# Loads of a tile's upper partitions issued by ACT, and a later start for the loads of weights

## The chip, the cores and the metric

The kernel runs on one core of a Trainium2 chip. The metric is the device time of one execution in microseconds (us); the time of a kernel is the median over several runs.

## The reference, cut to what matters

Three layers follow one another: attention in chunks with a few memory keys, a mixture of experts in which each token goes to two of eight, and a second one in which each token goes to one of eight.

```python
# attention: batch 4, heads 8, 768 positions, head size 64, chunks of 32
for c in range(nc):
    q_c = q[:, :, c_start:c_end]
    k_full = np.concatenate([mem_k, k[:, :, l_start:r_end]], axis=2)   # 16 left, 8 right, 8 memory keys
    v_full = np.concatenate([mem_v, v[:, :, l_start:r_end]], axis=2)
    scores = scale * np.matmul(q_c, k_full.transpose(0, 1, 3, 2))
    a = np.exp(scores - np.max(scores, axis=-1, keepdims=True))
    out[:, :, c_start:c_end] = np.matmul(a / (a.sum(-1, keepdims=True) + 1e-09), v_full)
x = out.transpose(0, 2, 1, 3).reshape(3072, 512)
# experts 1: noisy top 2 of 8;   h = max(x[mask] @ w1[e], 0);  out[mask] += weight * (h @ w2[e])
# experts 2: the largest of 8;   h = max(x[mask] @ w1[e], 0);  out[mask] = gate * (h @ w2[e])
```

## The kernel before

**Attention.** The 3072 tokens are 24 tiles of 128 tokens (NT = 24). The host lays out, for each tile, everything that attention needs of q, k and v in five arrays, `xa` to `xe`, and `load(t)` brings them into one of five buffers `X[t % LK]` (LK = 5) with five DMAs, all issued by SyncE: `xa` to partitions 0 to 31, `xb` to 32 to 63, `xc` to 64 to 127, `xd` to 64 to 95 and `xe` to 96 to 127. In a row they fill 2288, 1508, 736, 1552 and 772 floats. Two heads share the 128 partitions, and the columns hold the values (VN = 1040 for either half), the keys and the queries; what a half does not use is cleared once for each buffer by `clear` (VectorE and GpSimd), and `spread(t)` copies parts of the values along partitions on GpSimd.

**The order of the loop.** The loop over `t` is written out by hand and runs from 0 to 25; each engine executes its own instructions in this order. In iteration `t` stand: `clear(t + 1)` for the first buffers; `scores(t)`, 32 matmuls and on VectorE the maximum and the subtraction; `flip(t - 1)`, the transposes of the exponentials and their copy `et` on ACT; `exp(t)` on ACT; a step of the router `route` (VectorE above all) for a batch of six tiles; `values(t - 2)`, 32 matmuls, then `load(t + 3)` into the buffer that these matmuls were the last to read, then the division on VectorE, the split into a high and a low float16 part (VectorE, then GpSimd's subtraction), and the store of the tile to `X16` by SyncE; `spread(t)`; `turn(t - 3)`, the transposes of the tile and the copy `xt` on ACT; `logits(t - 4)`. So a load waits on its queue for the matmuls of `values`, and a store for GpSimd's subtraction. The loads of tiles 0 to 4 are issued ahead of the loop, and ACT then issues two small loads (noise and the router's weights).

**Zeroes and `wide`.** At `t == 2` VectorE writes a table `wide` for the router and a tile of zeroes, and SyncE stores the zeroes to the scratch tensors `L` (two stores) and `G`.

**Weights.** `Weights` brings the experts' weights in pieces of 128 partitions by 1024 floats (512 KB) into four staging buffers. `fill` issues loads, by SyncE, while fewer than `depth` pieces are staged; `high` converts a piece on ACT (L127) and `low` on VectorE (L128), and frees the buffer. In attention `depth` begins to grow at `t == 14`, by one in each iteration up to 4. The first conversion stands at `t == 24`.

**After attention** come the two mixtures of experts, matmuls of tokens gathered by GpSimd's DMAs; the change leaves their code alone.

Of the kernel before, what the change touches and what calls it, by code (L numbers as in the profile page):

```python
# [23 lines left out]
QN, KN, VN = 512, 736, 1040  # L24
QK = QN + KN
VC = VN // 4
XK, XQ, XU, XV = VN, VN + KN, VN + QK, VN + QK + QN
# [227 lines left out]
class Attention:  # L255
# [30 lines left out]
    def load(self, t):  # L286

        x = self.X[t % LK]  # L290
        for i, (p, n, o, e) in enumerate(((0, 32, 0, XU), (32, 32, 3 * VC, XU), (64, 64, XK, XQ),
                                          (64, 32, XU, XV + VN), (96, 32, XU, XV + VC))):
            self.nc.sync.dma_start(x[p:p + n, o:e], self.qkv[i][t])

    def spread(self, t):

# [925 lines left out]
def build(tc, xa, xb, xc, xd, xe, noise, wr, wg2, w1, w2, v1, v2, out):  # L1222
    nc = tc.nc
    with ExitStack() as top:
# [18 lines left out]
        def src(e):  # L1243
            v = (w1[e].rearrange("(p k) f -> p (k f)", k=4), w2[e].rearrange("(p k) d -> p (k d)", k=8))
            return lambda i, c: v[i][:, c * 1024:c * 1024 + 1024]

        with ExitStack() as ctx:
            wk = ctx.enter_context(tc.tile_pool(name="wk", bufs=2))
            ld = ctx.enter_context(tc.tile_pool(name="ld", bufs=1))
            at = Attention(tc, g, (xa, xb, xc, xd, xe), ld, wk)  # L1250
            at.ps = ctx.enter_context(tc.tile_pool(name="psa", bufs=1, space=PSUM))
            at.load(0)
            nc.scalar.preload_act_table_set("natural_log_exp_and_others")
            gates = at.gates(noise, wr)
            at.clear(0)
            constants(tc, g, ld)
            for t in range(1, LK):
                at.load(t)
            route = None
            for t in range(NT + 2):  # L1260
                if t + 1 < LK:
                    at.clear(t + 1)
                if t == 0:
                    next(gates)
                if t == 3:
                    at.wrh = next(gates)
                if t == 2:
                    g.wide = g.c.tile([128, 128, M], F16, name="wide")
                    nc.vector.tensor_copy(g.wide, g.iota[:, 0:128, None].to_broadcast([128, 128, M]))
                    z = ld.tile([128, NT * E], F32, name="zero")  # L1270
                    nc.vector.memset(z, 0.0)
                    for u in range(2):
                        nc.sync.dma_start(g.L.rearrange("(u p t) x -> u p (t x)", u=2, p=128)[u], z)
                    nc.sync.dma_start(g.G.rearrange("(p t) x -> p (t x)", p=128), z[:, 0:2 * NT])
                if t >= 14:
                    W.depth = min(W.depth + 1, 4)
                    if t == 14:
                        for e in range(E):
                            W.add((1, e), src(e))
                    W.fill()  # L1280
                if t < NT:
                    at.scores(t)
                if 0 < t <= NT:
                    at.flip(t - 1)
                if t < NT:
                    at.exp(t)
                if route and t < 25:
                    for _ in range(2 if t in (17,22) else 1):
                        next(route, None)
                if t >= 2:  # L1290
                    at.values(t - 2)
                if t < NT:
                    at.spread(t)
                if 0 <= t - 3 < NT - 2:
                    at.turn(t - 3)
                if t >= 4:
                    at.logits(t - 4)
                if t >= 4 and (t - 4) % TB == TB - 1:
                    route = at.route((t - 4) // TB)
                    next(route)  # L1300
                if t == 20:
                    m1 = Moe1(tc, g, dr)
                    m1.gather(0)
                if t == 22:
                    for b in range(m1.preps(0)):
                        m1.prep(0, b)
                if t >= 24 and W.may():
                    W.high()
                    W.low(nc.vector)
            m1.gates(0)  # L1310
# [143 lines left out]
def layouts(inp):  # L1454
    import numpy as np
    f = np.float32


    def split(x, y):

        return x.reshape(B, 2, 2, 2, *y)

    def pad(a):
        p = np.zeros((B, H, S + 40, D), f)
        p[:, :, 16:16 + S] = a
        return p
    q = split(inp["q"], (TB, 4, 32, D)).transpose(0, 4, 2, 7, 6, 1, 3, 5).reshape(NT, 128, QN)
    p = pad(inp["k"])
    k = np.stack([np.concatenate([x for c in range(4) for x in (p[:, :, 128 * j + 32 * c:128 * j + 32 * c + 32],
                                                                 inp["mem_k"])]  # L1470
                                 + [p[:, :, 128 * j + 128:128 * j + 152]], axis=2) for j in range(TB)], axis=2)
    k = split(k, (TB, KN // 4, D)).transpose(0, 4, 2, 6, 1, 3, 5).reshape(NT, 128, KN)
    p = pad(inp["v"])

    def values(w, c):

        w = split(w, (TB, c, 32, D)).transpose(0, 4, 3, 6, 5, 1, 2, 7)
        v = np.ones(w.shape[:-1] + (D + 1,), f)
        v[..., :D] = w
        return v.reshape(NT, 64, c * VC)  # L1480
    va = values(p[:, :, :S], 4)
    vb = values(np.concatenate([x for j in range(TB) for x in (p[:, :, 128 * j + 128:128 * j + 152], inp["mem_v"])],
                               axis=2), 1)
    seq = [b * TB + j for b, j in SEQ]
    k, q, va, vb = k[seq], q[seq], va[seq], vb[seq]
    vu = va[:, 32:].reshape(NT, 32, 4, VC)[:, :, ::-1].reshape(NT, 32, VN)
    qkv = [np.concatenate(x, axis=2) for x in ((va[:, 0:32], k[:, 0:32], q[:, 0:32]),
                                               (vb[:, 0:32], k[:, 32:64], q[:, 32:64]), (k[:, 64:],),
                                               (q[:, 64:96], vu), (q[:, 96:], vb[:, 32:]))]

    def rows(w):

        w = w.reshape(E, 4, 128, 128, 8).transpose(0, 2, 1, 4, 3)
        return np.ascontiguousarray(w).reshape(E, DM, F)

    def gate(w):
        return w.reshape(4, 128, -1).transpose(1, 0, 2).reshape(128, -1)
    return {
        **{"x" + "abcde"[i]: x for i, x in enumerate(qkv)},
        "noise": inp["moe_noise"].reshape(NT, 128, E)[seq].transpose(1, 0, 2).reshape(128, NT * E),  # L1500
        "wr": gate(np.concatenate([inp["moe_w_gate"], inp["moe_w_noise"]], axis=1)),
        "wg2": gate(inp["moe2_w_gate"]),
        "w1": rows(inp["moe_w1"]), "w2": inp["moe_w2"], "v1": rows(inp["moe2_w1"]), "v2": inp["moe2_w2"],
    }
# [30 lines left out]
```

## Time and profile before

| | |
|---|---|
| time, median of 3 runs | 1029.54 us (1027.92 to 1031.64) |
| the profiled execution's own time | 1027.09 us |
| its span in the profile | 1025.3 us |
| attention in it, first to last scores | 8.5 to 132 us |
| TensorE busy over the span | 952.6 us (93%) |
| VectorE, ACT, GpSimd busy | 49%, 38%, 47% |

The span is the time from the first to the last profiled instruction of one execution; the execution's own time has what lies around it as well. PE is TensorE, DVE VectorE, ACT ScalarE, POOL GpSimd, SP SyncE. The busy share is an average over stages with different limits, and a busy TensorE is not one at its peak, so the stage has to be read by itself.

### The profile page before, as it was taken

The numbers are of one execution on the slowest core, as the hardware profiler recorded it, in microseconds if no ns is written. First come the engines' busy times: TensorE is split into PE (matmuls) and PEld (weight loads), VectorE is DVE, ScalarE is ACT, GpSimd is POOL, SyncE is SP. The second block draws the span as 40 slices with busy tenths as digits, with TensorE's granted clock in tenths as the row PEclk, the third lists the DMA queues.
The fourth block names the chain that finished last, engine by engine and source line by source line (L and its number), as shares of the span: only waits on it lengthen the run. The fifth ranks groups of instructions, "written<-read, shape, count | busy, mean of one in ns | idle before, by whom it ended". The sixth has DMA issues, their size and how long they took to land.

```text
span 1025.3 us, 18840 instructions
## 1 busy us (share of the span) xinstructions
PE 952.6 (93%) x7303; PEld 568.2 (55%) x7303; DVE 499.7 (49%) x1032; ACT 386.0 (38%) x653; POOL 478.1 (47%) x484
## 2 busy tenths in 40 slices
PE   5898958999989999989999999998888998999998
PEld 4777845656545555445555555553464564555665
DVE  7689886642423443234233433483574265455511
ACT  2444444322423343234333333254324254445421
POOL 6755562334545454636455455345217245434321
PEclk9998979999999999999999999999989999999999
DMA  9999959745747686668668766498246689988720
GB/s 205 259 260 241 249 132 283 186 88 125 183 111 171 164 183 162 149 157 190 158 156 180 159 158 140 100 321 220 54 162 191 163 211 254 272 161 267 148 58 19
DMA packets 189218, 180.75 MB, mean 176 GB/s; under 512 B 152148, under 2 KB 153044, under 8 KB 188352
## 3 DMA queue, kind: packets, MB, share of 16 engines
q1 hardware_dynamic: 166736, 131.24, 54.6%
q0 software_dynamic: 21952, 48.07, 16.0%
q8 instruction: 60, 0.98, 0.4%
q14 instruction: 38, 0.31, 0.1%
q10 hardware_dynamic: 432, 0.15, 0.1%
HBM read 118.27 MB, written 39.53 MB: 154 GB/s over the span
## 4 chain that ended last, share of the span: by engine, by line
PE 30%; issue 13%; POOL 6%; DMA 5%; DVE 4%; ACT 1%; POOLq 0%; SPq 0%; DVEq 0%; ACTq 0%
PE ph L543 14%; PE py L554 14%; POOL x L1042 2%; POOL out_dram L1061 1%; DMA stage<-in_v_dram 1%; DMA Y<-y,t3y 1%; POOL xp L1014 1%; POOL gs L1014 1%; DMA xt<-x 1%; DVE w L128 1%; ACT w L127 1%; DMA xp<-Y,ter 1%; DMA xp<-Y,tbr 1%; DVE hT L546 1%; DVE ol L507 0%
## 5 line engine op out<-in xcount | busy, mean ns | idle before, releaser
L543 PE MATMUL ph<-xT,w 128*128 128x384 f16 (+3 forms) x2688 | 426.8, 318 | 26.4 <-DVE hT L546 15.5
L554 PE MATMUL py<-w,hT 128*128 128x512 f16 x1800 | 394.4, 379 | 1.4 <-ACT hT L545 1.1
L543 PEld LDWEIGHTS <-w 128*128 128x128 f16 x2688 | 262.9, 99 | 172.1 <-issue 29.8
L554 PEld LDWEIGHTS <-hT 128*128 128x128 f16 x1800 | 175.4, 98 | 209.2 <-ACT hT L545 1.6
L546 DVE SCALAR_TENSOR_TENSOR hT<-ph,hT 128x384 f16<-128x384 f32 (+3 forms) x224 | 115.6, 520 | 218.0 <-ACT hT L545 216.7
L128 DVE SCALAR_TENSOR_TENSOR w<-stage,w 128x1024 f16<-128x1024 f32 x128 | 165.9, 1300 | 72.8 <-ACT w L127 72.4
L545 ACT ACTIVATE hT<-ph 128x384 f16<-128x384 f32 (+3 forms) x224 | 103.1, 462 | 206.1 <-PE ph L543 205.8
L127 ACT ACTIVATE w<-stage 128x1024 f16<-128x1024 f32 x128 | 133.5, 1049 | 24.0 <-DMA stage<-in_v_dram 20.6
L654 ACT ACTIVATE y<-py,gs 128x512 f32<-128x512 f32 x48 | 32.9, 686 | 177.2 <-PE py L554 166.7
L675 DVE SCALAR_TENSOR_TENSOR x<-y,x 128x512 f16<-128x512 f32 x50 | 34.4, 688 | 123.8 <-ACT x L671 123.8
L657 POOL DMA_INDIRECT L<-l,t3y x43 | 44.7, 1038 | 98.7 <-DVE l L686 95.3
L657 POOL DMA_INDIRECT Y<-y,t3y x43 | 44.1, 1027 | 98.7 <-ACT y L654 88.2
L1061 POOL DMA_INDIRECT out_dram<-y,tbo x22 | 23.0, 1048 | 126.4 <-ACT y L1060 108.3
L316 PE MATMUL s<-x 128*64 128x64 f32 x768 | 49.5, 289 | 17.5 <-DMA x<-in_xe_dram 11.5
L611 POOL DMA_INDIRECT Y<-ol,late x48 | 56.0, 1166 | 16.4 <-issue 16.4
L316 PEld LDWEIGHTS s<-x 128*64 128x64 f32 x768 | 46.1, 208 | 19.0 <-POOL x L303 8.5
L1060 ACT ACTIVATE y<-py,gs 128x512 f32<-128x512 f32 x27 | 18.5, 686 | 90.6 <-PE py L554 59.9
L370 POOL TENSOR_TENSOR x<-x,x 128x512 f16<-128x512 f32 x24 | 29.5, 1228 | 47.2 <-DVE x L369 25.0
L585 POOL DMA_INDIRECT xg<-X,t3x x43 | 42.0, 978 | 15.1 <-issue 14.6
L585 POOL DMA_INDIRECT gs<-G,t3g x41 | 38.7, 944 | 12.5 <-issue 12.5
L1042 POOL TENSOR_TENSOR x<-xp 128x512 f32<-128x512 f32 x27 | 36.9, 1389 | 13.5 <-DVE xg L1045 9.9
L303 POOL COPY x<-x 24x780 f32<-24x780 f32 x48 | 41.0, 854 | 3.9 <-issue 1.3
(276 smaller groups left out, 702.1 us busy)
## 6 DMA issues: line engine op xcount, KB each, us to landing
stage<-in_w_dram SPq DMA_DIRECT2D x64, 512.0 KB, 4.9
stage<-in_v_dram SPq DMA_DIRECT2D x64, 512.0 KB, 5.9
x<-in_xa_dram SPq DMA_DIRECT2D x24, 286.0 KB, 8.2
X<-x SPq DMA_DIRECT2D x24, 256.0 KB, 4.8
x<-in_xd_dram SPq DMA_DIRECT2D x24, 194.0 KB, 5.9
x<-in_xb_dram SPq DMA_DIRECT2D x24, 188.5 KB, 5.0
x<-in_xc_dram SPq DMA_DIRECT2D x24, 184.0 KB, 7.5
x<-in_xe_dram SPq DMA_DIRECT2D x24, 96.5 KB, 7.2
```

The source lines that it names most:

```text
L127: nc.scalar.activation(hi, src, AF.Copy, scale=SW)
L128: return lambda v=nc.vector: v.scalar_tensor_tensor(lo, src, SW, hi, op0=OP.mult, op1=OP.subtract)
L303: self.nc.gpsimd.tensor_copy(x[p + 32:p + 56, d:d + 3 * VC], x[p:p + 24, s:s + 3 * VC])
L316: nc.tensor.matmul(s[o:o + 64, ch // 2, b], q[:, b, ch], k[:, b, 40 * ch:40 * ch + 64], start=True, stop=True)
L543: nc.tensor.matmul(p[:, :n], w1[:, a, k, f, :], xT[:, b, k, :n], start=(i == 0), stop=(i == 11))
L545: nc.scalar.activation(hT[:, 0, f, :n], p[:, :n], AF.Relu)
L546: nc.vector.scalar_tensor_tensor(hT[:, 1, f, :n], p[:, :n], 0.0, hT[:, 0, f, :n], op0=OP.max, op1=OP.subtract)
L554: nc.tensor.matmul(p[:m], hT[:, a, f, o:o + m], w2[:, c, f, :], start=(i == 0), stop=(i == 23))
L585: self.nc.gpsimd.indirect_dma_start(out=out, out_offset=None, in_=src, in_offset=IO(ap=idx, axis=0))
L611: st = nc.gpsimd.indirect_dma_start(out=self.Y, out_offset=IO(ap=idx[:, i:i + 1], axis=0), in_=z, in_offset=None, bounds_check=2 * N - 1, ...
L657: st = nc.gpsimd.indirect_dma_start(out=dst, out_offset=IO(ap=idx, axis=0), in_=src, in_offset=None, bounds_check=2 * N - 1, oob_is_err=False)
L1042: nc.gpsimd.tensor_tensor(s, x[:, :DM], x[:, DM:], op=OP.add)
```

## The change

In `load`, the three DMAs to partitions 64 to 127 are issued by ACT (`nc.scalar`), the two to partitions 0 to 63 by SyncE as before. The five stand in another order, in which the halves alternate, and the host's arrays are renamed to fit: `xb` is now what goes to partitions 64 to 95, `xc` what goes to 32 to 63, `xd` what goes to 64 to 127. What is transferred is the same. `wide` and the zeroes move from the iteration `t == 2` to `t == 6`. The loads of weights begin at `t == 18` instead of `t == 14`.

```diff
-        for i, (p, n, o, e) in enumerate(((0, 32, 0, XU), (32, 32, 3 * VC, XU), (64, 64, XK, XQ),
-                                          (64, 32, XU, XV + VN), (96, 32, XU, XV + VC))):
-            self.nc.sync.dma_start(x[p:p + n, o:e], self.qkv[i][t])
+        for i, (p, n, o, e) in enumerate(((0, 32, 0, XU), (64, 32, XU, XV + VN), (32, 32, 3 * VC, XU),
+                                          (64, 64, XK, XQ), (96, 32, XU, XV + VC))):
+            (self.nc.scalar if p >= 64 else self.nc.sync).dma_start(x[p:p + n, o:e], self.qkv[i][t])
...
-                if t == 2:
+                if t == 6:
                     g.wide = g.c.tile([128, 128, M], F16, name="wide")
...
-                if t >= 14:
+                if t >= 18:
                     W.depth = min(W.depth + 1, 4)
-                    if t == 14:
+                    if t == 18:
                         for e in range(E):
                             W.add((1, e), src(e))
...
-                                               (vb[:, 0:32], k[:, 32:64], q[:, 32:64]), (k[:, 64:],),
-                                               (q[:, 64:96], vu), (q[:, 96:], vb[:, 32:]))]
+                                               (q[:, 64:96], vu),
+                                               (vb[:, 0:32], k[:, 32:64], q[:, 32:64]),
+                                               (k[:, 64:],), (q[:, 96:], vb[:, 32:]))]
```

## Rows read from the trace of the kernel before

**Rows 1.** The page: DMA share in 40 equal slices of the span, in tenths.

```profile
DMA  9999959745747686668668766498246689988720
```

**Rows 2.** Stretches: busy us (instructions) by engine; then granted clock, DMA share, GB/s.

```profile
core 0: us, PE busy (x) PEld busy (x) DVE busy (x) ACT busy (x) POOL busy (x), PEclk, DMA share, GB/s
10.00:15.00 5.00, 2.55 (x43) 2.33 (x40) 2.90 (x5) 0.81 (x3) 4.70 (x6) 1.00 1.04 221
15.00:20.00 5.00, 3.64 (x41) 3.09 (x39) 4.25 (x9) 1.41 (x4) 1.55 (x2) 1.00 1.03 219
...
40.00:60.00 20.00, 20.00 (x388) 17.92 (x390) 13.46 (x31) 10.74 (x24) 14.31 (x16) 1.00 1.03 279
...
125.00:147.00 22.00, 13.66 (x263) 11.31 (x259) 20.07 (x66) 11.28 (x21) 14.02 (x13) 0.92 0.42 112
...
158.00:160.00 2.00, 2.00 (x19) 1.95 (x18) 1.84 (x3) 1.61 (x4) 0.00 (x0) 1.00 0.96 391
```

**Rows 3.** DMA issues from 152 to 160 us: KB each, median us to landing.

```profile
stage<-in_w_dram SPq DMA_DIRECT2D x5, 512.0 KB, 6.8
```

**Rows 4.** Waits of TensorE, to 36 us and from 36 to 131: us, times, longest.

```profile
PE s L316 <- DMA x<-in_xe_dram: 11.0, 2, 8.5
PE s L316 <- DMA x<-in_xd_dram: 5.1, 2, 3.7
...
PE misc L227 <- DVE two L428: 3.4, 1, 3.4
...
PE s L316 <- DMA x<-in_xd_dram: 0.8, 1, 0.8
PE s L316 <- DMA x<-in_xe_dram: 0.5, 1, 0.5
```

**Rows 5.** Timeline of TensorE: start, us, scores of tiles 0, 1, 2, 4, 5, 11.

```profile
8.51 2.09 PE L316 MATMUL s<-x 128*64 128x64 f32 x32 [8.51 <-DMA x<-in_xe_dram]
13.05 2.08 PE L316 MATMUL s<-x 128*64 128x64 f32 x32 [2.45 <-DMA x<-in_xe_dram]
...
17.54 2.10 PE L316 MATMUL s<-x 128*64 128x64 f32 x32 [1.36 <-DMA x<-in_xd_dram]
...
29.71 2.07 PE L316 MATMUL s<-x 128*64 128x64 f32 x32 [3.70 <-DMA x<-in_xd_dram]
...
35.17 2.05 PE L316 MATMUL s<-x 128*64 128x64 f32 x32
...
61.20 2.08 PE L316 MATMUL s<-x 128*64 128x64 f32 x32
```

**Rows 6.** Timeline of the links between those scores.

```profile
12.28 0.81 ACT L333 ACTIVATE e<-d 128x256 f32<-128x256 f32 x3 [10.23 <-DVE d L325]
...
15.06 1.12 PE L340 MATMUL pt<-ident,e 128*128 128x128 f32 x4
...
20.59 1.09 PE L356 MATMUL o<-x,et 128*32 128x130 f32 x32
...
23.49 1.16 POOL L370 TENSOR_TENSOR x<-x,x 128x512 f16<-128x512 f32 x1 [6.89 <-DVE x L369]
...
28.27 1.38 POOL L277 MEMSET x<- 64x1552 f32 x1
```

**Rows 7.** SyncE's issues: loads 15 and 25; then all of a kind, ns min/median/max.

```profile
10.63 0.31 SPq L293 DMA_DIRECT2D x<-in_xe_dram  x1
...
19.49 0.31 SPq L293 DMA_DIRECT2D x<-in_xe_dram  x1
...
L293 SPq DMA_DIRECT2D x<-in_xc_dram x24: 471/471/567, 1.7 to 121.2; - x24
L293 SPq DMA_DIRECT2D x<-in_xd_dram x24: 310/576/1280, 2.3 to 121.9; - x24
L293 SPq DMA_DIRECT2D x<-in_xe_dram x24: 310/419/608, 2.9 to 123.0; - x24
```

**Rows 8.** Timeline: the fourth load of weights, and the first conversions on ACT.

```profile
101.94 0.42 SPq L74 DMA_DIRECT2D stage<-in_w_dram  x1
...
140.94 1.99 ACT L127 ACTIVATE w<-stage 128x1024 f16<-128x1024 f32 x2
```

## The prediction

> **What bounds the kernel now.** I read the page first, then tables by stretch of time, then the waits of TensorE, then the timeline of the first 40 us. The page's row of DMA shares stands at 9 in the first five slices of 25.6 us: attention is the stage in which the DMA engines are full, and nothing later in the span is so for long [rows 1]. The change touches only this stage, from 0 to about 147 us.
>
> The table by stretch splits the stage. From 10 to 20 us nothing but loads of tiles is under way: 221 and 219 GB/s at a DMA share of 1.04 and 1.03, while TensorE works 2.55 and 3.64 us of 5. From 40 to 60 us TensorE is busy for all 20.00 us and the DMA share is 1.03 as well, now at 279 GB/s with the stores among the loads. From 125 to 147 us VectorE is busy 20.07 of 22 us and the DMA share is 0.42 [rows 2]. The reader is to see three bounds in turn: loads, then TensorE with the DMA just keeping up, then VectorE.
>
> One row decides what a faster load could be. From 158 to 160 us the traffic is loads of weights over all 128 partitions [rows 3], and they move 391 GB/s at a share of 0.96 [rows 2]. The loads of tiles, each within partitions 0 to 63 or 64 to 127, keep the engines as busy and move 220: the same engine takes nearly twice as long over each byte. So the limit of the first 20 us is not the number of busy engines; it goes with the half that is written.
>
> The waits of TensorE agree. Up to 36 us it waited for loads alone, 11.0 and 5.1 us; from 36 to 131 us only 0.5 and 0.8 us, and longer for VectorE, 3.4 us once [rows 4]. The timeline places them: scores of tile 0 start at 8.51, tile 1 at 13.05, tile 2 at 17.54 us, each released by a load, then tile 4 only at 29.71 and tile 5 at 35.17. From there no gap until tile 11 at 61.20: six tiles, 26.03 us, 4.34 us each [rows 5].
>
> **The change, part by part.** *Issue.* A tile is (32·2288 + 32·1508 + 64·736 + 32·1552 + 32·772)·4 B = 0.972 MB, and the two halves have 0.486 MB each. Three of its five loads go to ACT's queue. No byte is added. SP is relieved of, and ACT charged with, the medians of those three issues: 0.471 + 0.576 + 0.419 = 1.47 us a tile [rows 7].
>
> What it gains is a rate that the trace does not show: two queues, each confined to its half. Lower bound 220 GB/s (the two queues together do what one did), upper bound 391 (each half runs as alone, up to what a load over all partitions reached) [rows 2]. The engine that waits on one half can find a packet for the other in the second queue, which speaks for the upper row; that the packets alternate evenly is not shown, which speaks against its full value. I take the middle, 305. A tile then takes 0.972/0.305 = 3.19 us instead of 0.972/0.220 = 4.42, so 1.23 us less.
>
> Scores of tile 2 need three tiles: 3·1.23 = 3.7 us earlier. From there to tile 4 the chain is engine work in a fixed order: transposes, values of tile 0 at 20.59, GpSimd's subtraction at 23.49, four spread copies, the clearing of buffer 4 at 28.27 for 1.38 us, scores at 29.71 [rows 5, 6]. GpSimd had idled 6.89 us before 23.49, so it can start earlier, and all links move together: 3.7 us. At 391 GB/s the loads would give 3·(4.42 − 2.49) = 5.8, but scores of tile 1, then at 13.05 − 3.9 = 9.2, and the 2.08 and 1.12 us behind them keep tile 2 from starting before 12.4, which leaves 5.1. Both ends: 0 and 5.1.
>
> *Does it last?* From tile 5 TensorE needs a tile every 4.34 us. A tile and its store of 0.262 MB at 391 GB/s (0.67 us) take 4.42 + 0.67 = 5.09 us now, which only the five tiles loaded ahead make good, and 3.19 + 0.67 = 3.86 at 305. It lasts if the rate is above 0.972/(4.34 − 0.67) = 265 GB/s. Past 61 us the stage is paced by VectorE; there only the waits of 0.5 and 0.8 us for loads go [rows 4]: 1.3 us.
>
> *ACT.* Its work is 10.74 us in 20 [rows 2], 2.33 a tile; (20/4.34 = 4.6 tiles); with 1.47 it is 3.80, under 4.34. Break-even is (4.34 − 2.33)/3 = 0.67 us an issue; the longest on SP took 1.28, behind a full queue [rows 7]. A load of tile t+3 waits on ACT for the matmuls of values of tile t−2, and behind it stand the copy of the transposed tile, the next copy of `et` and the next exp. Those matmuls start as soon as the transposes of the tile are done, before that tile's exp has its input, so I cost the wait at nothing; what hides it is VectorE's maximum and subtraction. Without that cover it is a part of the 1.09 us of those matmuls. SP keeps the stores behind the other two loads and loses only entries.
>
> *Zeroes and `wide`*, from the third to the seventh tile: one copy, one memset and three small stores move on VectorE and SP. VectorE is busy 4.25 us of 5 at the old place and 13.46 of 20 at the new [rows 2]. Nothing either way, bounds plus and minus 1 us.
>
> *Weights.* Four loads of 512 KB move by four tiles; the fourth now goes out at 101.94 us and ACT first touches one at 140.94 [rows 8]. Some 20 us later is still early enough, under the cover of the last tiles. They leave tiles 17 and 20, whose waits I have counted, and meet tiles 20 to 23: nothing at 305 GB/s, but at 220 they cost there what they save before.
>
> *Sum.* 3.7 + 1.3 = 5.0 us. The profiled execution took 1027.09 us around a span of 1025.3; 1027.09 − 5.0 = 1022.1. The median of the runs is 2.45 above that execution, so 1024.5. What follows attention starts earlier by as much, with its order unchanged.
>
> **Rivals.** *The two queues do as one.* The busy share is 1.03 already [rows 2]; if engines meet at the same half at the same time, as they must when loads of one half are all that one queue holds, a second queue only changes the order. Then nothing is gained: 1029.5. Against it: the engines are free to be out of step, and with stores among the loads the rate was 279. This is also what the Trainium skill says: SBUF — State Buffer, section "Can I just issue two DMAs to hit both halves?", has two concurrent loads at partitions 0 and 64 only 6% faster than one, and DMA: Bandwidth & Descriptors, section "Issuing engines are not separate DMA queues", has a second issuing engine save only issue time. By that the rate would be 233 GB/s, the three tiles 0.8 us earlier and the time 1028.8. No run here shows it yet; the port table that the Trainium skill has on the first of these pages, section "Door 1: The DMA port swizzle (why `[64,N]` ≈ `[32,N]`)", by which either half reaches half of the ports, agrees with 220 against 391 [rows 2].
>
> *ACT is held at the head of its stream*, the one that ends on the other side. All fifteen loads of tiles 0 to 4 on ACT stand ahead of its first exp, which started at 12.28 us. SP issued its fifteenth load at 10.63 but its last, of tile 4, at 19.49, held back by a full queue [rows 6, 7]. If ACT is held as long, exp ends at 20.6, the first transposes start there instead of at 15.06, and scores of tile 2 follow 1.1 later, at 21.8 instead of 17.54: 4.2 us late, down the same chain. Time 1033.7. It decides once exp starts after 15.6 us (17.54 − 1.12 for the transposes − 0.81 for itself). For it: the issues of a full queue. Against: ACT's queue holds 128 rows a tile, not 192, and drains faster if the rate rises.
>
> *ACT becomes the bound.* At 0.9 us an issue ACT has 2.33 + 2.7 = 5.03 us a tile, 0.7 over TensorE, on six tiles 4.1 us: it eats the 3.7, and the time is about 1028.6.
>
> **Numbers.** Forecast 0.55, queues as one 0.25, ACT held 0.13, ACT the bound 0.07. A difference under 0.3%, 3.1 us, can hardly be told from none in runs that lie 3.7 us apart (1027.92 to 1031.64). The forecast's own range goes from 1022.0 (5.1 + 1.3, and 1.1 because tile 4 need not take 35.17 − 29.71 = 5.46 us but 4.34) to 1026.0 (265 GB/s: 3·0.75 + 1.3). The whole range takes in two things more. If the chain between tiles 2 and 4 does not stay whole and TensorE alone paces it from 12.4 us on, tile 5 starts at 12.4 + 3·4.34 = 25.4 instead of 35.17; with the 1.3 that is 11.1 us, 1018.4, and less the 1.6 us by which the fastest run shown lies under the median, about 1017. Above, queues as one with the 2.1 us by which the slowest lies over it give 1032; most of the ACT-held case is left out. Faster 0.55; same 0.27 (queues as one, and a little of ACT as the bound); slower 0.18 (ACT held, the rest).
>
> **What would show it.** In the stretch from 5 to 15 us, over 265 GB/s at a share of about 1; scores of tile 2 before 15 us and of tile 5 near 31.5; tiles 5 to 11 still 4.34 us apart; exp of tile 0 before 12.3; no waits of TensorE for tiles 17 to 23. Wrong at the first step: 220 GB/s and tile 2 at 17.5. Wrong at ACT: exp of tile 0 after 15.6, issues of 0.7 us and more, or gaps of TensorE that `et` ends.

## Result, and the profile after

The change made the kernel slower by half a per cent: 1033.18 us against 1026.88 us (medians of 20 runs each), a ratio of 1.0057, 95% interval 1.0039 to 1.0076. One of the changed kernel's runs took 1932.45 us, where the other 19 lie between 1028.40 and 1041.41, and the ratio is without it (the median of the 19 is 1032.71). The forecast was 1024.5, its range ended at 1032. The profiled execution of the changed kernel took 1041.41 us and so lies 8 us over its own median; what it shows of the first 156 us is used here, what it loses after them is not put down to the change (from the first expert matmul to the last it took 877.7 us, before 872.8).

Stretches of the changed kernel, with the columns of [rows 2]:

```profile
10.00:15.00 5.00, 2.46 (x40) 2.12 (x36) 3.71 (x7) 0.00 (x0) 4.70 (x5) 1.00 1.02 222
15.00:20.00 5.00, 0.00 (x0) 0.00 (x0) 0.00 (x0) 0.37 (x2) 1.38 (x1) 1.00 1.03 229
...
40.00:60.00 20.00, 17.60 (x345) 15.76 (x342) 13.59 (x28) 9.19 (x20) 14.46 (x15) 1.00 0.96 257
125.00:147.00 22.00, 16.82 (x294) 14.26 (x287) 18.52 (x66) 10.82 (x25) 14.88 (x16) 0.84 0.81 212
```

Two things are to be seen. The loads hardly went faster: 222 and 229 GB/s at a share of 1.02 and 1.03, where [rows 2] have 221 and 219. And from 15 to 20 us TensorE and VectorE did nothing at all and ACT 0.37 us, while the loads went on. TensorE's waits to 36 us and from 36 to 131 us (as in [rows 4]):

```profile
PE s L316 <- DMA x<-in_xe_dram: 8.3, 1, 8.3
PE pt L340 <- ACT e L333: 6.9, 1, 6.9
PE s L316 <- POOL x L277: 5.0, 2, 3.9
...
PE misc L227 <- DVE two L428: 4.0, 1, 4.0
PE xp L383 <- ACT xt L384: 2.6, 3, 1.4
```

The loads are waited for once, for tile 0. The 6.9 us for ACT's exp and the 2.6 us for its copy `xt` are new. ACT's timeline (DMA issues and the first exp) shows why:

```profile
16.58 0.32 ACTq L293 DMA_DIRECT2D x<-in_xe_dram  x1
18.74 0.36 ACTq L283 DMA_DIRECT2D noi<-in_noise_dram  x1
19.14 0.45 ACTq L247 DMA_DIRECT2D wrf<-in_wr_dram  x1
19.63 0.81 ACT L333 ACTIVATE e<-d 128x256 f32<-128x256 f32 x3 [15.93 <-DMA x<-in_xb_dram]
```

The first exp starts at 19.63 us instead of 12.28 [rows 6], behind ACT's fifteenth load of a tile and two small loads. The scores follow (tiles 1, 2, 4, 5, 7, 8, 9; compare [rows 5]):

```profile
11.52 2.06 PE L316 MATMUL s<-x 128*64 128x64 f32 x32 [1.12 <-POOL x L277]
21.54 2.11 PE L316 MATMUL s<-x 128*64 128x64 f32 x32
...
34.00 2.12 PE L316 MATMUL s<-x 128*64 128x64 f32 x32 [3.89 <-POOL x L277]
39.67 2.04 PE L316 MATMUL s<-x 128*64 128x64 f32 x32
...
48.33 2.04 PE L316 MATMUL s<-x 128*64 128x64 f32 x32
53.68 2.04 PE L316 MATMUL s<-x 128*64 128x64 f32 x32
59.48 2.04 PE L316 MATMUL s<-x 128*64 128x64 f32 x32
```

Tile 1 is 1.5 us early, tile 2 is 4.0 us late, tile 5 4.5 us late. Then tiles 7 to 8 and 8 to 9 take 5.35 and 5.80 us instead of 4.34. That is where the zeroes now stand, in the changed kernel's timeline of SyncE and of ACT:

```profile
48.23 1.22 SPq L1273 DMA_DIRECT2D L<-zero  x2
49.50 1.69 SPq L1274 DMA_DIRECT2D G<-zero  x1
```

```profile
50.04 1.16 ACTq L293 DMA_DIRECT2D x<-in_xd_dram  x1
51.24 0.60 ACTq L293 DMA_DIRECT2D x<-in_xe_dram  x1
51.88 1.02 ACT L384 ACTIVATE xt<-xp 128x1024 f16<-128x1024 f16 x1 [2.73 <-POOL x L370]
...
56.53 0.47 ACTq L293 DMA_DIRECT2D x<-in_xd_dram  x1
...
57.68 1.02 ACT L384 ACTIVATE xt<-xp 128x1024 f16<-128x1024 f16 x1 [3.59 <-PE o L356]
```

Issues are stretched on both engines, and the copy `xt` stands behind ACT's. TensorE's transposes wait for that copy in both tiles, 2.4 of the 2.5 us that these two tiles lose:

```profile
52.96 0.61 PE L383 MATMUL xp<-ident,x 128*128 128x128 f16 x8 [0.97 <-ACT xt L384]
...
58.76 0.61 PE L383 MATMUL xp<-ident,x 128*128 128x128 f16 x8 [1.43 <-ACT xt L384]
```

At tile 23 the kernel is 8.8 us late (scores at 139.0 against 130.2), at the first expert matmul 9.1 (156.2 against 147.1).

**What an issue waits for.** The compiled program gives each DMA of SyncE and ACT one of eight completion semaphores (counters that a landing DMA raises), in turn, over both engines together; a DMA is issued only when the one eight places earlier has landed. GpSimd's DMAs have eight others and no place in this rotation. The trace has the semaphore of each DMA and the time of each landing. In the changed kernel (places counted from 0):

| place | engine | DMA, issued at | waits until this has landed, at |
|---|---|---|---|
| 23 | ACT | `xe` of tile 4, 16.58 | place 15, ACT's `xb` of tile 3, 16.56 |
| 24 | ACT | noise, 18.74 | place 16, SyncE's `xa` of tile 3, 18.72 |
| 25 | ACT | router's weights, 19.14 | place 17, ACT's `xd` of tile 3, 17.45 |

So ACT's stream could reach its first exp only when three loads of tile 3 were in. The lateness that the prediction read in [rows 7] as a full queue was this wait: there the load eight places before the last one landed at 19.48 us, and the last went out at 19.49. In the kernel before, nearly all of these waits were SyncE's (ACT issued the two small loads at the very start), and no computing stood in that stream. The same wait is in the two tiles at the zeroes: ACT's issue at 56.53 follows the landing, at 56.51, of a load that SyncE had issued at 51.29, behind its last store of zeroes. It does not explain single issues that take up to 1.8 us where most take 0.3 to 0.6; what stretches those is not shown.

### The profile page after: what moved, and what is told of

The parts are those of the page before. It is cut to its first block, busy times and chain, and to the rows that moved or that the text cites. A ratio compares the mean times of both kernels' runs of the same rounds, so it can differ in the third digit from the quotient of the medians.

```text
span 1039.4 us, 18864 instructions
## 1 busy us (share of the span) xinstructions
PE 954.8 (92%) x7303; PEld 568.8 (55%) x7303; DVE 503.0 (48%) x1032; ACT 384.9 (37%) x653; POOL 477.2 (46%) x484
## 4 chain that ended last, share of the span: by engine, by line
PE 28%; issue 14%; POOL 7%; DMA 5%; DVE 4%; ACT 1%; POOLq 0%; DVEq 0%; ACTq 0%; SPq 0%
PE py L554 14%; PE ph L543 13%; POOL x L1042 2%; DMA xt<-x 2%; DMA stage<-in_v_dram 1%; POOL out_dram L1061 1%; POOL gs L1014 1%; POOL xp L1014 1%; DVE w L128 1%; DMA Y<-y,t3y 1%; DMA xp<-Y,tbr 1%; ACT w L127 0%; DVE hT L546 0%; POOL L L657 0%; DVE ol L507 0%
## 5 line engine op out<-in xcount | busy, mean ns | idle before, releaser
L316 PEld LDWEIGHTS s<-x 128*64 128x64 f32 x768 | 46.3, 209 | 16.5 <-POOL x L303 8.3
L1042 POOL TENSOR_TENSOR x<-xp 128x512 f32<-128x512 f32 x27 | 35.8, 1350 | 13.5 <-DVE xg L1045 9.9
```

The lines of the kernel that those rows point to most:

```text
L316: nc.tensor.matmul(s[o:o + 64, ch // 2, b], q[:, b, ch], k[:, b, 40 * ch:40 * ch + 64], start=True, stop=True)
L1042: nc.gpsimd.tensor_tensor(s, x[:, :DM], x[:, DM:], op=OP.add)
```

## The experiments

The timed runs. Columns: ratio to the kernel before, as timed on the same chip, with its interval (the chips differ: the median of before goes from 1025.93 us for e1 to e3 to 1039.31 for e5 to e8); then, in us and from one profiled execution each, start of the first exp, of the scores of tile 5, from there to tile 11, start of the scores of tile 23, of the first expert matmul. Such starts scatter: e5 is the kernel before up to tile 14, and its tile 5 starts 0.65 us later.

| kernel | ratio | exp | tile 5 | 5 to 11 | tile 23 | experts |
|---|---|---|---|---|---|---|
| before | 1 | 12.3 | 35.2 | 26.0 | 130.2 | 147.1 |
| after | 1.0057 [1.0039, 1.0076] | 19.6 | 39.7 | 28.8 | 139.0 | 156.2 |
| e1 split alone | 1.0064 [1.0038, 1.0091] | 19.9 | 40.6 | 26.0 | 136.5 | 153.4 |
| e2 both moves alone | 1.0043 [1.0021, 1.0065] | 12.2 | 34.5 | 27.1 | 133.4 | 150.9 |
| e3 after, head by SyncE | 1.0039 [1.0013, 1.0065] | 12.2 | 35.3 | 29.4 | 135.5 | 152.8 |
| e5 weights alone | 1.0012 [0.9989, 1.0035] | 12.0 | 35.8 | 26.1 | 132.1 | 149.9 |
| e6 zeroes alone | 0.9998 [0.9971, 1.0025] | 12.3 | 36.2 | 27.5 | 132.6 | 149.6 |
| e7 order alone | 0.9982 [0.9957, 1.0007] | 11.8 | 35.2 | 26.0 | 130.2 | 147.1 |
| e8 split in the loop | 1.0064 [1.0027, 1.0101] | 12.1 | 36.2 | 31.0 | 136.9 | 155.2 |
| e11 split at the head | 1.0024 [0.9996, 1.0053] | 19.6 | 39.9 | 26.0 | 134.9 | 151.8 |
| e12 e8, zeroes first | 1.0081 [1.0055, 1.0107] | 12.3 | 37.9 | 26.7 | 134.4 | 153.5 |
| e14 e8, zeroes by GpSimd | 0.9995 [0.9967, 1.0023] | 12.0 | 35.7 | 26.8 | 131.7 | 149.6 |
| e13 clear early, alone | 1.0002 [0.9981, 1.0023] | 14.7 | 31.2 | 28.7 | 128.5 | 145.7 |
| e10 order and clear early | 0.9964 [0.9940, 0.9987] | 14.0 | 30.2 | 27.2 | 126.3 | 143.5 |

The last column less 147.1 and the change of time (ratio less 1, times the median of before) agree within 3.3 us in every row. The intervals are 1.9 to 3.8 us wide to either side, so that most of these differences may be nothing; what happens to them after attention wasn't followed.

**e1, the split alone; e2, the two moves alone; e3, the changed kernel with tiles 0 to 4 by SyncE.**

```diff
e1: the change, with wide and zeroes at t == 2 and the weights from t >= 14
e2: the kernel before, with wide and zeroes at t == 6 and the weights from t >= 18
e3: the change, with
-            (self.nc.scalar if p >= 64 else self.nc.sync).dma_start(
+            (self.nc.scalar if p >= 64 and t >= LK else self.nc.sync).dma_start(
```

> The issue by two queues and the new order of the loads, with the zeroes back at the third tile and the weights back at the 15th. Theory head (ACT's first exp stands behind fifteen loads and two small ones, and everything of attention follows it): exp of tile 0 near 19.6 us, scores of tile 5 near 39.7 instead of 35.2, the time 4 to 5 us over the kernel before. Theory moves (what costs is the zeroes in TensorE's stretch and the weights beside the last loads): scores of tile 5 late as well, but the time within 2 us of the kernel before, because the lost start is made up where loads were short. Theory loop (the three issues in every tile make ACT late all along): tiles 5 to 11 more than 4.5 us apart here too.

> The kernel before with the zeroes and the table moved to the seventh tile and the weights to the 19th, all loads on one queue in the old order. Theory head: the time of the kernel before within 1.5 us, exp of tile 0 at 12.3 us. Theory moves: 2 to 6 us over it, lost between tiles 5 and 9 and at tiles 22 and 23. Theory loop: as theory head.

> The changed kernel, but the loads of tiles 0 to 4, ahead of the loop, are all issued by SyncE in the new order; in the loop the upper halves stay on ACT. Theory head: exp of tile 0 back near 12.3 us, scores of tile 5 near 35 us, the time 4 to 5 us under the changed kernel, so within 2 us of the kernel before. Theory loop: exp back at 12.3 us, yet tiles 5 to 11 take 28 us or more instead of 26, and the time stays 2 us or more over the kernel before. Theory moves: 2 us or more over the kernel before too, but with the loss at the zeroes (tile 7 to 9) and at the last two tiles.

e1 has the late exp and the whole loss with tiles 5 to 11 at 4.34 us: ACT's three issues a tile did not slow the loop there. It differs from the changed kernel by the two moves alone, and of these only that of the zeroes and `wide` acts before tile 14, so that move makes the 28.8 us of the changed kernel. e2 has a loss without any split. e3 takes the head's loss away (exp at 12.2, tile 5 at 35.3) and is still slower than before: tiles 5 to 11 take 29.4 us, tile 8 to 9 alone 6.8. So no one theory carries the loss, and the losses do not add; why the loop of e1 keeps its pace is taken up below, with e8.

**e4 and e9, the rate by itself.** Both only load, and store at the end; their times, 151.92 and 196.51 us, are not the kernel's.

> Loads alone, nothing computed, so the time says nothing of the kernel: six stretches, each ended by a clearing of the five buffers, which waits for the loads. (1) five tiles on one queue in the old order, (2) five tiles on two queues as changed, (3) five tiles on one queue in the order in which the halves alternate, (4) the lower halves alone on one queue, (5) ten loads of 512 KB over 128 partitions on one queue, (6) the same on two queues. Theory as-one (loads are served one after another, whichever queue they come from): 215 to 235 GB/s in (1), (2), (3) and (4) alike, and 380 to 420 in (5) and (6) alike. Theory side by side (the rate of the prediction, which did not show because ACT was held): (2) above 265 GB/s, (1) and (4) near 220.

In e4 whole buffers were cleared between the stretches, one every 4.0 us, which paced some of the loads, and most neighbouring stretches overlapped. One result stands all the same: from 62 to 74 us only loads of the third stretch were under way, the new order by SyncE alone, and they moved 262 to 275 GB/s at a DMA share of 0.96 to 1.07. Two of the six rows (the last two columns are the DMA share and GB/s):

```profile
66.00:68.00 2.00, 1.88 (x1) 0.00 (x0) 1.00 0.99 262
70.00:72.00 2.00, 1.89 (x1) 0.00 (x0) 1.00 0.96 267
```

A tile landed every 3.62 us, which is 268 GB/s. In e9 each stretch starts when the one before has landed:

```diff
+    for u in range(LK):   # gate
+        nc.vector.tensor_copy(seen[:, 2 * u:2 * u + 1], X[u][:, XK:XK + 1])
+        nc.vector.tensor_copy(seen[:, 2 * u:2 * u + 2], X[u][:, XU - 1:XU + 1])
...
+    tiles(lower + upper, nc.sync); tiles(turn, nc.scalar); tiles(turn, nc.sync)
+    tiles(lower + upper, nc.scalar); tiles(lower, nc.sync); tiles(upper, nc.sync)
+    full(nc.sync); full(nc.scalar)
```

> Nothing is computed: eight stretches of loads of five tiles each (4.86 MB; the fifth and sixth stretch only one half), and every stretch starts when the one before has landed. One: SyncE alone, old order. Two: SyncE and ACT, new order. Three: SyncE alone, new order. Four: SyncE and ACT, old order. Five and six: the lower, the upper half alone. Seven and eight: loads over all 128 partitions, by one and by two queues. The theory that two queues do as one and only the order of the halves counts: one 218 GB/s, two and three alike at 230 to 235, four no more than 235, five and six 218, seven and eight alike near 391. The rival, that two queues are faster where nothing else holds them: two at 265 GB/s or more, three at 220.

One row inside each of its eight stretches, in that order (last three columns: granted clock, DMA share, GB/s):

```profile
30.00:45.00 15.00, 0.97 (x6) 0.00 (x0) 1.00 1.03 221
50.00:65.00 15.00, 0.97 (x6) 0.00 (x0) 1.00 1.03 233
75.00:90.00 15.00, 1.29 (x8) 0.00 (x0) 1.00 1.02 235
95.00:110.00 15.00, 0.97 (x6) 0.00 (x0) 1.00 1.02 237
119.00:125.00 6.00, 0.65 (x4) 0.00 (x0) 1.00 1.05 214
135.00:140.00 5.00, 0.80 (x5) 0.00 (x0) 1.00 1.04 207
151.00:160.00 9.00, 1.13 (x7) 0.00 (x0) 1.00 1.02 412
165.00:175.00 10.00, 1.28 (x8) 0.00 (x0) 1.00 1.03 415
```

Old order by one queue 221. Two queues 233, and the same new order by one queue 235: the second queue gives nothing. Old order by two queues 237: either way of mixing the halves gives 5 to 7% here. One half alone 207 and 214; all 128 partitions 412 and 415, by one queue or two. The Trainium skill, SBUF — State Buffer, "Can I just issue two DMAs to hit both halves?", has two loads at once, one in either half, 6% faster than a single one; these rows have 5% over one queue with the halves in blocks, 9 to 13% over one half alone. The Trainium skill, DMA: Bandwidth & Descriptors, "Issuing engines are not separate DMA queues", has a second issuing engine save only issue time; the rows agree where the halves are mixed as well by one queue (235 and 233) and over all partitions (412 and 415).

The third row is the same loads, in the same order, by the same queue as in e4, at 235 instead of 268. One thing that differs in the traces is how the 16 landing events of one load lie: in e4 they are spread over 1.2 us and overlap those of the next load, which mostly goes to the other half; in e9 they are spread over 0.7 to 0.8 us and mostly don't overlap. That in e4 the DMA engines were out of step and so wrote to both halves at once is a reading of this, not shown: no run varies it alone. So how much mixing the halves can give stays open between these two; it takes no second queue.

**e5 and e6, the moves one by one; e7, the new order by SyncE alone; e8, the split in the loop alone.**

```diff
e5: the kernel before, with the weights from t >= 18
e6: the kernel before, with wide and zeroes at t == 6
e7: the change without its moves, and
+            self.nc.sync.dma_start(x[p:p + n, o:e], self.qkv[i][t])
e8: the change without its moves, and
+            (self.nc.scalar if p >= 64 and t >= LK else self.nc.sync).dma_start(
```

> The kernel before with one edit: the loads of weights begin with the 18th tile. The theory that the weights carry the loss of the two moves (they lie beside the loads of the last tiles and a later piece is late): the last tiles' scores and the first expert matmul 3 to 4 us later than before (150 to 151 us against 147.1), everything up to tile 17 as before, ratio 1.003 to 1.004. The rival, that the zeroes and the wide table carry it: tile 23 at 130.2 and the first expert matmul at 147 as before, ratio 1.000.

> The kernel before with one edit: the wide table and the zeroes move from the third to the seventh tile. The theory that the weights carry the loss: up to 1 us between tiles 5 and 11 (26.0 us before), first expert matmul at 147 to 148, ratio 0.999 to 1.001. The rival, that the zeroes and the table carry it: tiles 5 to 11 over 27 us, first expert matmul at 150 or later, ratio 1.003 to 1.004.

> All five loads of a tile issued by SyncE as before, but in the new order in which the halves alternate; the table, the zeroes and the weights at their old places. The theory that one queue's packets follow in order of issue, so that only loads of both halves under way together gain: in the loads alone one alternating queue moved about 267 GB/s against 220; then three tiles take 3 x (4.42 - 3.64) = 2.3 us less, scores of tile 2 at about 15.2 and of tile 5 at about 33 us, ratio about 0.998. The rival, that the order is of no account in one queue: 216 to 221 GB/s from 5 to 20 us, scores of tile 2 at 17.5, ratio 1.000.

> Loads of tiles 0 to 4 all issued by SyncE in the new order, those of the later tiles split between SyncE and ACT; the table, the zeroes and the weights at their old places. The theory that the head of ACT's stream and the moves carry all of the loss: exp of tile 0 at 12.3 us, tile 5 at 35, tiles 5 to 11 in 26.0 us, first expert matmul at 147, ratio 0.999 to 1.001. The rival, that issuing in the loop costs ACT its own time: tiles 5 to 11 in 27 us or more, later tiles up to 3 us late, ratio 1.002 to 1.004.

In either move's trace the first expert matmul is 2.5 to 2.8 us late (of this 0.65 and 1.0 by tile 5, where the former is scatter), with the weights at the last tiles, with the zeroes between tiles 9 and 10 (5.6 us); neither alone is told from no change by its time, so how e2's 0.43% divides stays open. The order alone has tile 2 at 16.5 instead of 17.5, a gain that is gone by tile 5, and no time that could be told from before: of the expected 2.3 us, 1.0 came. e8 went against the theory: with the head in order, tiles 5 to 11 take 31.0 us and the whole loss is back. Its waits of TensorE from 36 to 135 us, and of SyncE's issues to 60 us:

```profile
PE s L316 <- DMA x<-in_xc_dram: 10.9, 7, 2.4
...
SPq L293 <- DMA x<-in_xb_dram: 18.5, 8, 6.4
```

TensorE waits for loads that SyncE issues, and SyncE waits for loads that ACT issues. The timeline of the first of these:

```profile
24.83 0.32 SPq L1274 DMA_DIRECT2D G<-zero  x1
...
27.25 0.32 ACTq L293 DMA_DIRECT2D x<-in_xb_dram  x1
...
31.60 0.33 SPq L293 DMA_DIRECT2D x<-in_xa_dram  x1
```

31.60 is the first load of tile 5 on SyncE; ACT's at 27.25 is the first of tile 6. In the compiled program the former has place 36 in the rotation and the latter place 28: tile 5's load waited until a load of the next tile had landed. For tiles 7 to 11 the first load on SyncE waits in the same way for ACT's first load of its own tile, so the halves follow each other: six of the seven first loads of tiles 5 to 11 go out within 0.1 us of the landing that they wait for. In e1, which splits these tiles in the same way, the DMAs of its head stand in another order, and for each of the seven the DMA eight places earlier had landed 0.8 to 6.6 us before. So the same split cost nothing in that loop: what it costs depends on which DMAs come to stand eight places apart.

**e11, the split at the head alone; e12 and e14, e8 with another rotation.**

```diff
e11: the change without its moves, and
+            (self.nc.scalar if p >= 64 and t < LK else self.nc.sync).dma_start(
e12: e8, with the zeroes (memset and three stores) behind the loads of tile 0
e14: e8, with the zeroes at t == 2 by GpSimd
-                    nc.sync.dma_start(g.G.rearrange("(p t) x -> p (t x)", p=128), z[:, 0:2 * NT])
+                    nc.gpsimd.dma_start(g.G.rearrange("(p t) x -> p (t x)", p=128), z[:, 0:2 * NT])
...
```

> Only the loads of tiles 0 to 4 are split between SyncE and ACT; those in the loop are all issued by SyncE, in the new order; table, zeroes and weights at their old places. The theory that ACT is held by its fifteen loads until DMAs issued before them have landed, and that this alone costs the whole loss: exp of tile 0 at 19.9 us, tile 4 at 34.7, tile 5 at 40.6, later tiles 4.34 us apart up to tile 11, first expert matmul 3 to 6 us late, ratio 1.004 to 1.006. The rival, that the late head is made up later and the loss needs the issues in the loop: first expert matmul at 147 to 148, ratio 0.999 to 1.002.

> The split in the loop alone, as in the run before (tiles 0 to 4 by SyncE, later ones split, ratio 1.0064), but the three stores of zeroes stand behind the loads of tile 0 instead of in the third iteration. No load changes its engine or its place among the loads. In the list as built every DMA waits for one eight places earlier in a rotation that runs over both engines; with the zeroes in the third iteration the first load of tile t on SyncE waits there for ACT's first load of tile t+1, with the zeroes first it does not. The theory that this rotation makes the loss of the split in the loop: scores of tile 5 at 35 to 36 us, tiles 5 to 11 in 26 to 27 us instead of 31.0, waits of TensorE for loads under 2 us between 36 and 135 instead of 10.9, ratio 0.999 to 1.002. The rival, that ACT's own time for the issues or a lower rate of two queues makes it: tiles 5 to 11 in 30 us or more, ratio 1.005 to 1.008.

> The split in the loop alone (tiles 0 to 4 by SyncE, later ones split), with the three stores of zeroes at their old place in the third iteration but issued by GpSimd, whose DMAs take no place in the rotation that SyncE's and ACT's share. The theory that the rotation makes the loss in the loop: tile 5 at 35 to 36 us, tiles 5 to 11 in 26 to 27 us, waits of TensorE for loads between 36 and 135 us under 3 us instead of 10.9, first expert matmul at 148 to 151, ratio 1.000 to 1.003. The rival, that ACT's own time for the issues makes it: tiles 5 to 11 in 30 us or more, first expert matmul at 153 or later, ratio 1.005 to 1.008.

e11: exp, tile 5 and the first expert matmul (4.7 us late) are where the theory of the held head has them; the time, 1.0024, is only half of what it expected, and its interval holds no change as well as 1.005. e12: the loop went from 31.0 to 26.7 us, as the rotation has it; but the stores now lay among the first loads, tile 1 started at 14.7 instead of 12.7, and the time did not improve, against its expectation (of the 6.4 us at the first expert matmul 2.8 are there by tile 5; about half comes after tile 11 and wasn't followed). (What its expectation says of the waits in e8 holds word for word for tile 5 only; for later tiles it is the same tile, as above.) e14 has that rotation without the disturbed head. TensorE's waits for loads from 36 to 135 us, and the first load of tile 5 on SyncE:

```profile
PE s L316 <- DMA x<-in_xc_dram: 1.8, 2, 1.4
...
22.84 0.31 SPq L293 DMA_DIRECT2D x<-in_xa_dram  x1
```

22.84 instead of 31.60, 1.8 us of waits instead of 10.9, 26.8 us for tiles 5 to 11, and a ratio of 0.9995. ACT issues as many loads as in e8, at the same places in its stream. So what cost the loop was the shared rotation, not ACT's time for the issues and not a lower rate of two queues; of the 5.0 us 0.8 stay, and the first expert matmul is 2.5 us late in this trace, which its time does not show.

**e10 and e13, each buffer cleared an iteration earlier.** In e7 tile 4 still started at 29.39 us, after 3.88 us for GpSimd's clearing of the fifth buffer.

```diff
-                if t + 1 < LK:
-                    at.clear(t + 1)
+                if t == 0:
+                    at.clear(1)
+                if t + 2 < LK:
+                    at.clear(t + 2)
```

> All loads by SyncE in the new order, table, zeroes and weights at their old places, and each buffer is cleared one iteration earlier (the fifth at the third iteration instead of the fourth). With the order alone the scores of tile 4 waited 3.9 us for GpSimd's clearing of the fifth buffer. The theory that this clearing sets the start of the steady loop: scores of tile 4 at about 26 instead of 29.4 us, tile 5 at 32, ratio 0.995 to 0.998. The rival, that the chain of engines up to tile 4 is late anyway: tile 4 at 29 us, ratio 0.998 to 1.001.

> The kernel before with one edit: each buffer is cleared one iteration earlier; loads in the old order, by SyncE. The theory that the clearing of the fifth buffer sets the start of the loop and the order of the halves adds about 1 us: scores of tile 4 at 26 to 27 us instead of 29.7, first expert matmul at 144 to 145, ratio 0.996 to 0.998. The rival, that it needs the faster loads of the new order: tile 4 at 28 us or later, first expert matmul at 146 to 147, ratio 0.999 to 1.001.

e10 is e7 with this edit, e13 the kernel before with it. Scores of tile 4 in e10 and in e7:

```profile
25.62 2.10 PE L316 MATMUL s<-x 128*64 128x64 f32 x32 [0.44 <-issue]
```

```profile
29.39 2.06 PE L316 MATMUL s<-x 128*64 128x64 f32 x32 [3.88 <-POOL x L277]
```

e10 is faster than both kernels: 1033.19 against 1037.31 us for the kernel before on the same chip, 0.9964 [0.9940, 0.9987]. It has no split. In e13 tile 5 is 4.0 us early as well (31.2), but at tile 11 1.2 us are left (60.0 against 61.2): in the old order the loads cannot keep a lead. Tile 4 itself, at 26.8, came as the theory of its expectation had it; the time is that of the rival.

## Why the prediction was wrong

**The rate was the step that failed first.** "I take the middle, 305" between 220 and 391. Measured: 222 and 229 in the kernel from 10 to 20 us (the same order by one queue, in e10, has 236 and 244 there), 233 against 221 by itself. By 233 three tiles come 3 · (0.972/0.221 − 0.972/0.233) = 0.7 us earlier, not 3.7. The upper bound is real (412 over all partitions), but it belongs to one load over both halves. The rival "the two queues do as one" said this, and the 6% that the Trainium skill gives (SBUF — State Buffer, the section named above) was the better number. That the mixed loads can go faster, as the step argued, e4 shows with its 268, but with one queue, and the head of the kernel did not get there.

**The issues' hold was the step that cost most in the trace.** The rival "ACT is held at the head of its stream" had the mechanism: exp at 19.63 lies beyond its point of decision, 15.6, and tile 2, worked out at 21.8 us, came at 21.54. That the numbers meet is luck. ACT's fifteenth load went out at 16.58 us and not, as the rival had it, at 19.49, and the small loads behind it made up the difference; and 1033.7 beside 1033.18 compares 4.2 us over 1029.54 with 6.3 over 1026.88, moves included. Without the moves e1 is 5.4 us over before by the medians, 6.6 by the ratio. Nor did the hold set the sign alone: e3, without it, is slower too (1.0039, interval above 1), and e11, with it alone, can't be told from no change. The rival had 0.13 because I took SyncE's late issues for a full queue and held that ACT's shorter queue would drain sooner. The limit that the trace shows there is a count of eight DMAs, common to both engines, and not the length of either queue. I also counted the fifteen loads, but not the two small ones behind them: 3.05 us from the issue of the fifteenth to the exp.

**The chain from tile 2 to tile 4** moved as one, as the step had it: 12.46 us against 12.17. One reading beside it was wrong: TensorE had not "waited for loads alone" up to 36 us. The 3.7 us at tile 4, which [rows 5] put down to a load, ended with GpSimd's clearing (28.27 + 1.38 = 29.65 [rows 6]); the loads of tile 4 had landed by 26.89. That its last link, the clearing, could be taken out of it was in the range ("if the chain does not stay whole") and is what e10 does.

**Whether an earlier start lasts** was asked rightly: by that step a tile and its store take 5.09 us in the old order, against TensorE's 4.34, and in e13 a lead of 4.0 us shrank to 1.2 over six tiles.

**ACT's time for the issues** was right at nothing where nothing held them: e1 keeps 4.34 us a tile, e14 as a whole 0.9995. What the step left out, when it put the wait on ACT at nothing, is that an issue on ACT also waits for the landing of DMAs that SyncE issued. In the changed kernel this, with the stretched issues, is the 2.4 us for which TensorE waited for the copy `xt`.

**Zeroes, wide and weights at nothing** were wrong together: e2, 1.0043. The zeroes are three DMAs of little size, and the changed kernel lost (5.35 − 4.34) + (5.80 − 4.34) = 2.5 us at tiles 7 to 9, beside them; e1, without the moves, lost nothing there. How much of it comes from their three places of eight and how much from stretched issues (1.69 us for the last of the three) is not shown.

**The sum.** Of the 9.1 us at the first expert matmul 4.5 are the head (tile 5), 2.5 the two tiles at the zeroes, the other 2.1 lie from tile 9 on and were not divided between the weights and the split. The time shows 6.3 (1033.18 − 1026.88; by the ratio 5.9); where the other 3 us went after attention stays open.

## What to carry to other kernels

Before an engine that computes is given DMAs to issue, read in the compiled program what each issue waits for: here it was the landing of another engine's transfer eight places back, and everything behind it in the stream waited too. Splitting loads by issuer bought no rate here; loads over all partitions had nearly twice the rate (no run loads the tiles so), and mixing the halves in one queue gave what gain there was, 6% in e9 and 21% in e4. A stage that starts earlier is worth something only where the next limit lets it keep the lead: the early clearing gained with the mixed order and not without it.

## What was not expected of the hardware

A load confined to partitions 0 to 63 moved 214 GB/s and one to 64 to 127 207 GB/s, at a DMA share of 1.05 and 1.04; loads over all 128 partitions moved 412 at 1.02. Mixing both halves brought 233 to 237 in e9, by one queue or two, and 268 over 12 us in e4, by one; in neither do the rates of the two halves add. The rotation of eight is a property of the compiled program, not of the chip; the runs show its price, 5 us over six tiles (31.0 against 26.0), with not a byte more to move.
